# A planned list of instructions: the length over which each engine is held to the plan's order

## The chip, the cores and the metric

The kernel runs on one core of a Trainium2 chip. The metric is the device time of one execution, in microseconds, the median of three runs. The core has five engines with an instruction stream each: TensorE (PE in the profile, its weight loads PEld), VectorE (DVE), ScalarE (ACT), GpSimd (POOL), and SyncE (SP), which issues nearly all DMAs. Each engine works through its own stream in order, and waits on semaphores for the others.

## The reference

Inputs are q, k, v of shape (8, 8, 576, 64) (batch, head, position, width), g_norm of 64, and two weight matrices, 512x2048 and 2048x512. All is float32.

```python
kv  = einsum('bhsd,bhse->bhde', k, v)
out = einsum('bhsd,bhde->bhse', q, kv)
x   = out / sqrt(mean(out * out, -1) + 1e-6) * g_norm      # then heads side by side: (8, 576, 512)
X   = real(fft(fft(x, axis=1), axis=2))
u   = x + X
un  = (u - mean(u)) / sqrt(var(u) + 1e-6)                  # over the last axis
y   = u + maximum(un @ w_ch1, 0) @ w_ch2
```

## The kernel before

Matmuls on TensorE are done in a rounded float32 format, and where that is too coarse each operand is split in a high and a low part and multiplied in three passes (high by high, high by low, low by high). That makes three matmuls out of one in the Fourier and in the feed-forward stages.

The program has two parts. The **first part** takes all eight batches through attention and the Fourier stage, and a share of the feed-forward work along with them. The **second part** does the rest of the feed-forward work in the order in which its loops are written. Only the first part matters here. Its operations, by the names of their PSUM tiles and their lines:

- `ps_k` (L574): k^T v of a head pair, from tiles `km`, `vm` (loads at L553) and the rest rows `kr`, `vr` (loads at L562).
- `ps_q` (L643): q transposed by a matmul with an identity; `qt` is loaded at L618, and one row of it, 2 KB, at L624. ACT copies the result to `fq` (L647).
- `ps_o` (L669): attention output. ACT copies it (L686) and squares it (L691), DVE sums the squares (`ss`, L696), POOL multiplies by the gain (L709).
- the fold: DVE (L774, L785), ACT and POOL (L792, L801) make sums and differences of the rows, and their high and low parts `xh` and `xl`.
- `ps_f` at L816: Fourier over positions, 9 matmuls for each of 4 groups (36 a batch); ACT and DVE copy it to `pt` (L830, L834).
- `ps_f` at L851: Fourier over the width, 36 matmuls a batch; ACT and DVE make `me` and `pm` (L863, L871), POOL adds them to x (L883, L886), SP stores it to `u_scr` (L897).
- `ps_t` (L942): x transposed; ACT and DVE write `unTh` and `unTl` (L951, L954), which SP stores, 1 MB each, to `unT_scr` (L1062).
- `ps_h` (L424) and `acc` (L442): the two feed-forward products, with hidden tiles `hh` (ACT, L434) and `hl` (DVE, L437); a partial result goes to `part_scr` (L1056).
- `ps_s` (L494): spare matmuls, 45 pairs whose result nobody reads, which the plan puts where TensorE would otherwise be idle.

All these take their PSUM tile from one ring of 8 banks, `p8`.

The order is made in two steps. First a `Plan` (class at L92) collects each operation with its engine, a cost in ns, a rank, the operations it comes after and the buffers that it takes from rings. `Plan.run` (L155) then walks through a model of time: whenever an engine is free it takes the ready operation of the lowest rank whose buffers are free, and emits its instructions. Second, the framework's scheduler takes the program that was emitted, and orders each engine's stream anew by its own model of time. What keeps it from this is `Plan.pin` (L129): for every instruction emitted at a planned time up to `PIN_UNTIL` it adds a dependence, without a semaphore, on the last such instruction of the same engine. Instructions emitted later carry no such dependence, and the scheduler may let any of them overtake any other of the same engine, as far as data and buffers allow. `PINNED` names the engines for which it is done: all five. Times in `Plan.run` are ns of the plan's own model, which are not those of the chip: the pinned stretch ends at about 90 us of the trace.

Of the kernel before, what the change touches and what calls it, by code (L numbers as in the profile page):

```python
# [46 lines left out]
SPARE_FROM = 12000  # L47


PIN_UNTIL = 95000  # L50
PINNED = {
    mybir.EngineType.PE, mybir.EngineType.DVE, mybir.EngineType.Activation,
    mybir.EngineType.Pool, mybir.EngineType.SP,
# [35 lines left out]
class Plan:  # L89
# [39 lines left out]
    def pin(self, emit, now):  # L129
# [6 lines left out]
        for i in traced[start:]:  # L136
            if i.engine not in self.pinned or now > PIN_UNTIL:
                continue
# [1298 lines left out]
```

## Time and profile before

| | us |
|---|---|
| median of three runs | 1025.26 |
| lowest, highest | 1024.71, 1025.57 |
| the profiled execution | 1022.79 |
| its span | 1021.0 |
| TensorE busy | 1002.3 (98%) |
| VectorE, ScalarE, GpSimd busy | 475.3, 324.8, 314.4 |

The span is the time from the first to the last instruction that the profile shows; the execution's own time has 1.79 us more. The profile's chain of waits is the path that ended last, followed back from the last instruction to whatever released each step. A window of it lists pieces in order of time, with start, length, engine, tile, line and the count of instructions. The view of waits sums, for an engine's line, the time it stood idle and what ended that. A row with SPq is a DMA being issued; the time in it is that of the issue, not of the transfer. The last store of x in the first part is issued at 327 us of the span; the second part is most of the rest.

### The profile page before, as it was taken

What the parts mean: (1) busy time and instruction counts of PE and PEld (TensorE: products, weight loads), DVE (VectorE), ACT (ScalarE), POOL (GpSimd) and SP (SyncE); (2) the same over time, 40 slices, a digit from 0 to 9 for tenths busy, and PEclk for the clock granted to TensorE, in tenths of its full rate; (3) what the DMA queues carried; (4) which work ended last, traced back from release to release, by engine and by line L of the source; (5) the groups of instructions that cost most, each with busy time, mean ns of one, the idle gap of its engine ahead of it and who ended that gap; (6) DMA issues with size and microseconds to landing.
All of it is one profiled execution on the core that took longest, in us unless ns stands there. A gap on an engine that the chain in (4) does not pass through costs nothing.

```text
span 1021.0 us, 15425 instructions
## 1 busy us (share of the span) xinstructions
PE 1002.3 (98%) x6070; PEld 844.0 (83%) x6070; DVE 475.3 (47%) x847; ACT 324.8 (32%) x657; POOL 314.4 (31%) x328
## 2 busy tenths in 40 slices
PE   5999999999999999999999999999999999999997
PEld 5898888889888888888888888888888888888886
DVE  4897656654788879997131313131221311311211
ACT  2666556554644434344221202121121120210110
POOL 0526768775675132235722303020020010100000
PEclk9999999999999999999999999999999999999999
DMA  9989778664346775645553514230320400400101
GB/s 250 212 230 282 181 209 258 162 170 131 137 163 213 268 253 191 236 129 170 161 179 86 180 59 150 82 125 0 141 67 1 165 21 1 165 0 1 42 1 42
DMA packets 109260, 140.74 MB, mean 138 GB/s; under 512 B 51854, under 2 KB 76482, under 8 KB 104580
## 3 DMA queue, kind: packets, MB, share of 16 engines
q1 hardware_dynamic: 105652, 132.28, 41.9%
q0 software_dynamic: 1920, 6.29, 1.9%
q10 hardware_dynamic: 1616, 1.18, 0.5%
q8 instruction: 48, 0.79, 0.3%
q14 instruction: 24, 0.20, 0.1%
HBM read 88.33 MB, written 51.40 MB: 137 GB/s over the span
## 4 chain that ended last, share of the span: by engine, by line
PE 97%; DMA 1%; ACT 0%; POOL 0%; DVE 0%; issue 0%; SPq 0%; DVEq 0%; POOLq 0%
PE ps_h L424 38%; PE acc L442 38%; PE ps_o L669 4%; PE ps_f L816 4%; PE ps_f L851 4%; PE ps_k L574 3%; PE ps_s L494 2%; PE ps_q L643 2%; PE ps_t L942 2%; DMA qt<-in_q_dram 1%; PE ps_w L383 1%; DMA vm<-in_v_dram 0%; POOL x L883 0%; ACT x L686 0%; DVE uu L1324 0%
## 5 line engine op out<-in xcount | busy, mean ns | idle before, releaser
L424 PE MATMUL ps_h<-unTh,w 128*128 128x512 f32 x1152 | 356.6, 391 | 1.2 <-ACT fq L647 1.2
L442 PE MATMUL acc<-w,hh 128*128 128x512 f32 x1152 | 345.5, 390 | 0.0
L437 DVE SCALAR_TENSOR_TENSOR hl<-ps_h,hh 128x512 fp32r<-128x512 f32 x144 | 99.1, 688 | 371.8 <-ACT hh L434 367.5
L442 PEld LDWEIGHTS acc<-w,hh 128*128 128x128 f32 x1152 | 215.1, 188 | 44.3
L424 PEld LDWEIGHTS ps_h<-unTh,w 128*128 128x128 f32 x1152 | 214.8, 188 | 44.8 <-ACT fq L647 1.4
L434 ACT ACTIVATE hh<-ps_h 128x512 fp32r<-128x512 f32 x144 | 85.8, 596 | 454.0 <-PE ps_h L424 439.2
L424 PE MATMUL ps_h<-unTl,w 128*128 128x512 f32 x576 | 224.3, 389 | 0.0
L442 PE MATMUL acc<-w,hl 128*128 128x512 f32 x576 | 213.5, 389 | 0.0
L424 PEld LDWEIGHTS ps_h<-unTl,w 128*128 128x128 f32 x576 | 108.1, 188 | 22.6
L442 PEld LDWEIGHTS acc<-w,hl 128*128 128x128 f32 x576 | 108.1, 188 | 22.6
L1271 POOL DMA_INDIRECT uu<-u_scr,rowidx x24 | 23.2, 968 | 285.1 <-DVE uu L1324 177.9
L709 POOL TENSOR_TENSOR x<-x,gb 96x512 f32<-96x512 f32 (+1 forms) x42 | 55.0, 1330 | 45.7 <-ACT x L686 40.3
L1290 POOL TENSOR_TENSOR uu<-uu,up 128x512 f32<-128x512 f32 x36 | 45.7, 1298 | 45.2 <-ACT up L1287 45.2
L1234 POOL TENSOR_TENSOR w<-wap,w 128x512 fp32r<-128x512 f32 x18 | 26.4, 1467 | 75.3 <-ACT w L1233 69.1
L669 PEld LDWEIGHTS ps_o<-kvt,fq 64*96 64x96 f32 (+1 forms) x864 | 40.9, 162 | 5.7 <-issue 4.0
L1324 DVE SCALAR_TENSOR_TENSOR uu<-acc,rs_yb,uu 128x512 f32<-128x512 f32 x36 | 25.2, 744 | 42.5 <-PE acc L442 42.5
L669 PE MATMUL ps_o<-kvt,fq 64*96 64x64 f32 (+1 forms) x864 | 44.4, 248 | 0.0
L696 DVE TENSOR_REDUCE ss<-ps_o 96x8 f32<-96x512 f32 (+1 forms) x48 | 32.0, 682 | 26.5 <-ACT ps_o L691 26.3
L792 POOL TENSOR_TENSOR xe<-ab 96x256 f32<-96x256 f32 (+1 forms) x46 | 38.0, 845 | 18.7 <-DVE ab L785 17.9
L816 PE MATMUL ps_f<-cs,xh 96*128 96x290 f32 (+1 forms) x192 | 39.0, 300 | 0.0
L1278 DVE BATCH_NORM_STATS2 bst<-uu 128x6 f32<-128x512 f32 x36 | 24.5, 687 | 29.0 <-DMA uu<-u_scr,rowidx 19.8
L851 PE MATMUL ps_f<-cd,pt 128*96 128x258 f32 (+1 forms) x288 | 37.8, 285 | 0.0
(114 smaller groups left out, 1022.4 us busy)
## 6 DMA issues: line engine op xcount, KB each, us to landing
raw<-in_moe_w_ch_dram SPq DMA_DIRECT2D x32, 512.0 KB
unT_scr<-unTh SPq DMA_DIRECT2D x9, 1024.0 KB
unT_scr<-unTl SPq DMA_DIRECT2D x9, 1024.0 KB
part_scr<-part SPq DMA_DIRECT2D x36, 256.0 KB
unTh<-unT_scr SPq DMA_DIRECT2D x9, 1024.0 KB
unTl<-unT_scr SPq DMA_DIRECT2D x9, 1024.0 KB
up<-part_scr SPq DMA_DIRECT2D x36, 256.0 KB
out_dram<-uu SPq DMA_DIRECT2D x36, 256.0 KB
```

The costliest lines, as they stand in the source:

```text
L424: nc.tensor.matmul(ps, w[c][:, kc * P : (kc + 1) * P], unT[a][:, kc, :], start=(idx == 0), stop=(idx == 3 * KC - 1),)
L434: nc.scalar.activation(hh, ps, AF.Relu)
L437: nc.vector.scalar_tensor_tensor(hl, ps, 0.0, hh.bitcast(F32), ALU.max, ALU.subtract)
L442: nc.tensor.matmul(acc, hpair[a][:, i * P : (i + 1) * P], w[c], start=(first and n == 0), stop=(last and n == 2),)
L574: nc.tensor.matmul(ps.t[s * D : (s + 1) * D, pr * D : (pr + 1) * D], km[:, s, j, :] if j < 4 else kr[:, h, :], vm[:, s, j, :] if j < 4 els ...
L669: nc.tensor.matmul(pss[s].t[:n, at : at + D], fqs[side].t[half, m, :n], kvt.t[half, m], start=True, stop=True,)
L696: nc.vector.tensor_reduce(ss.t[0][:n, :, t, s::2], pss[s].t[:n].rearrange("p (u m e) -> p u m e", u=2, e=D), AX.X, ALU.add,)
L709: nc.gpsimd.tensor_tensor(v_, v_, gb[:n].unsqueeze(1).to_broadcast([n, H, D]), ALU.mult)
L792: nc.gpsimd.tensor_tensor(o[:, s], a[:, 0], a[:, 1], ALU.subtract if s else ALU.add)
L816: nc.tensor.matmul(ps.t[:, :NS], xs[t].t[a][:n, part, ch * P : (ch + 1) * P], cs[:n, part, c, t, :], start=(idx == 0), stop=(idx == 8),)
L851: nc.tensor.matmul(ps.t[:n, :ND], pt.t[a][:, part, ch, offs[t] : offs[t] + n], cd[:, part, c, ch, :], start=(idx == 0), stop=(idx == 5),)
L1290: nc.gpsimd.tensor_tensor(us[j][i], us[j][i], part, ALU.add)
```

## The change

`PIN_UNTIL` goes from 95000 to 260000, so the dependence is added for everything emitted in the first 260 us of the plan's time.

```diff
-PIN_UNTIL = 95000
+PIN_UNTIL = 260000
```

Both programs have the same instructions. Their places differ in one stretch of each engine's stream, on TensorE from about the 605th to the 1870th of 5295, which is about 90 to 267 us of the trace; before and after it the streams are the same.

On TensorE, between the attention products and the next feed-forward block, about 115 us in the trace. Names are those of the list above; `128x97 x4` is the shape of the result and the number of equal instructions in a row. Lines with - are before, with + after:

```order
 L669 MATMUL ps_o<-kvt,fq 96x64 x16
-L574 MATMUL ps_k<-vm,km 64x64 x6
-L942 MATMUL ps_t<-ident,x 128x97 x2
-L942 MATMUL ps_t<-ident,x 128x96 x2
+L942 MATMUL ps_t<-ident,x 128x97 x4
+L942 MATMUL ps_t<-ident,x 128x96 x4
 L643 MATMUL ps_q<-ident,qt 128x96 x4
-L574 MATMUL ps_k<-vm,km 64x64 x2
-L574 MATMUL ps_k<-vr,kr 64x64 x2
-L574 MATMUL ps_k<-vm,km 64x64 x3
-L942 MATMUL ps_t<-ident,x 128x97 x2
-L942 MATMUL ps_t<-ident,x 128x96 x2
```

Before, the products of k and v and the transposes alternate in pieces of two to eight; after, each of them stands whole, the transposes of eight and the ps_k of ten or twenty. A little further on, before, four ps_t stand between the ps_o that follow the acc; after, they stand ahead of the acc. And the last of the 45 spare pairs, which was the last thing ahead of an acc at 90 us, stands between the last two groups of eight ps_q just ahead of the ps_h of 130 us.

On TensorE, in the Fourier stage of the next batch, about 148 us in the trace:

```order
 L851 MATMUL ps_f<-cd,pt_1958 96x258
-L574 MATMUL ps_k<-vm,km 64x64 x2
-L851 MATMUL ps_f<-cd,pt_1957 96x258 x2
-L574 MATMUL ps_k<-vm,km 64x64 x5
-L574 MATMUL ps_k<-vr,kr 64x64 x2
 L851 MATMUL ps_f<-cd,pt_1957 96x258 x2
 L851 MATMUL ps_f<-cd,pt_1958 96x258
```

The ps_k that stood among the 36 matmuls of L851 now come after them, after 16 ps_o and eight ps_t; the 36 stand in one run. The same holds for the 36 at about 181 us.

On SP, at about 204 us in the trace, where two stores of unT (128x2048, 1 MB each) stand next to loads. Before:

```order
L1062 DMA unT_scr<-unTh 128x2048
L1062 DMA unT_scr<-unTl 128x2048
L618 DMA qt<-in_q_dram 96x24x64
L624 DMA qt<-in_q_dram 1x8x64
L553 DMA km<-in_k_dram 128x2x256
L553 DMA vm<-in_v_dram 128x2x256
L1056 DMA part_scr<-part 128x512
```

The same place after the change:

```order
L618 DMA qt<-in_q_dram 96x24x64
L624 DMA qt<-in_q_dram 1x8x64
L553 DMA km<-in_k_dram 128x2x256
L553 DMA vm<-in_v_dram 128x2x256
L1062 DMA unT_scr<-unTh 128x2048
L1056 DMA part_scr<-part 128x512
L1062 DMA unT_scr<-unTl 128x2048
L618 DMA qt<-in_q_dram 96x24x64
```

Here the loads of q, k and v go ahead of the two stores. Elsewhere on SP it is the other way: of the km and vm loads that were issued from 116.9 to 128.2 us ahead of two such stores, four, and vr with them, stand behind the stores after the change.

On DVE, ACT and POOL the moved instructions lie in stretches of about 180, 230 and 135 places; the last copies to `pt` and `pm` go ahead of the next batch's fold on DVE, and the copies of ps_t are not parted any more.

## The prediction

> **What bounds the kernel now.** I read the chain that ended last first, because it names the engine whose time has to shrink. Its share by engine stands on the page:
>
> ```profile
> PE 97%; DMA 1%; ACT 0%; POOL 0%; DVE 0%; issue 0%; SPq 0%; DVEq 0%; POOLq 0%
> ```
>
> TensorE is the chain nearly from end to end, so time can be won only where it stands still or runs slower than it must. The window view shows how much of each stretch it is busy, for the part that was pinned already and for the part that the change pins anew (columns: length, then busy time and count of PE, PEld, DVE, ACT, POOL, the granted clock, DMA share, GB/s):
>
> ```profile
> 20.00:90.40 70.40, 70.40 (x861) 60.24 (x858) 56.62 (x98) 38.77 (x86) 24.50 (x37) 1.00 0.95 245
> 90.40:266.60 176.20, 173.22 (x1703) 151.37 (x1702) 103.15 (x190) 100.61 (x237) 126.04 (x137) 1.00 0.69 191
> ```
>
> In the pinned stretch TensorE is never idle. In the unpinned one it is idle for 176.20 - 173.22 = 2.98 us; the clock is full in both, so no gain or loss can come from it there. The waits of TensorE in that second stretch are three (total, times, longest, us):
>
> ```profile
> PE ps_h L424 <- ACT fq L647: 1.2, 1, 1.2
> PE ps_k L574 <- DMA vm<-in_v_dram: 1.0, 1, 1.0
> PE ps_t L942 <- POOL x L883: 0.4, 1, 0.4
> ```
>
> Plain waiting is thus worth 2.6 us at most. What else can be won lies inside the busy time: an operation that is broken into short pieces takes longer than the same operation in one run. The prices of whole runs come from the chain (start, us, count), at places where nothing breaks them. The trace counts a ps_k matmul twice, so its 60 here are 30 in the program.
>
> ```profile
> 204.34 2.63 PE ps_k L574 x60
> ...
> 209.23 1.50 PE ps_o L669 x32
> ...
> 249.19 1.99 PE ps_t L942 x24
> 251.18 2.40 PE ps_o L669 x32
> 253.58 0.81 PE ps_q L643 x8
> ...
> 285.53 4.30 PE ps_f L851 x36
> ```
>
> **The change part by part.** Instructions and their number stay; only positions move, between about 90 and 267 us of the trace on every engine. So I price the five places where TensorE loses something: the elapsed time in the chain less the same matmuls at the prices above.
>
> **First place, 115 to 131 us:**
>
> ```profile
> 115.33 0.50 PE ps_k L574 x12
> ...
> 121.82 2.09 PE acc L442 x9
> 123.92 0.88 PE ps_o L669 x12
> 124.80 0.48 PE ps_t L942 x4
> 125.28 2.37 PE ps_o L669 x50
> 127.65 0.06 issue
> ```
>
> From 115.33 to 121.82 are 6.49 us, in which eleven pieces alternate: sixty ps_k (2.63), twenty ps_t (1.99 x 20/24 = 1.66) and eight ps_q (0.81), 5.10 in whole runs. So 1.39 are lost in breaks; the new order runs them in seven pieces. From 123.92 to 127.65 are 3.73, for 64 ps_o (3.00) and four ps_t (0.33): 0.40 lost, and the new order has no ps_t between them. Then ps_h waits 1.2 for the bank that the last fq copy frees (the row above). In the new order ps_h waits for another bank, that of the spare matmuls, so this wait goes. What is late next is the pair of ps_q whose banks hang on the square sums (L696) of the two ps_o before them; that is the same evacuation one step earlier, and I count it as covered by the first ps_q and the spare matmuls ahead. Sum 1.39 + 0.40 + 1.2 = 3.0 won.
>
> The spare pair itself:
>
> ```profile
> L494 PE MATMUL ps_s<-still x90: 387/397/588, 13.4 to 90.4; 128*128 128x512 f32 x90
> ```
>
> The last pair goes from 90 us to just ahead of that ps_h. It costs about half a us wherever it stands on the path, so it gives and takes the same: zero. If it stands in a moment when TensorE would wait anyway, half a us more is won.
>
> **Second place, 146 to 165 us:**
>
> ```profile
> 146.32 0.88 PE ps_k L574 x20
> 147.20 1.12 PE ps_f L851 x8
> 148.32 0.26 PE ps_k L574 x2
> ...
> 153.98 0.11 DVE pm L871
> ...
> 164.63 0.40 PE acc L442
> ```
>
> From 146.32 to 153.98 are 7.66 us, for forty ps_k (1.75), 36 ps_f (4.30) and four ps_o (0.19), 6.24 whole: 1.42 lost in breaks. Two ps_k records that stand alone take 0.26 where two sixtieths of 2.63 make 0.09. The new order runs the 36 ps_f as one, so I take back 1.4. From 153.98 to 164.63 are 10.65, for sixty ps_o (2.81), 24 ps_t (1.99), forty ps_k (1.75) and sixteen ps_q (1.62), 8.17 whole: 2.48 lost, and the chain runs through DVE, POOL and ACT there. These engines still have to do the same copies and adds. They start earlier, since ps_f ends earlier, but POOL is nearly full:
>
> ```profile
> 150.00:175.00 25.00, 24.33 (x307) 20.59 (x306) 13.37 (x26) 15.80 (x37) 22.30 (x24) 1.00 0.88 253
> ```
>
> With 22.30 of 25 busy, POOL can close little. Between nothing and 2.48 I take a third, 0.8. Sum of the place: 2.2.
>
> The Trainium skill (TensorE: Matmul & The Clock Gate, Step-by-step: what each phase is for) says that weights for the next tile load while the present matmul streams, by which a break between two independent operations would cost nothing. This trace disagrees: 0.26 for the two ps_k that stand alone, three times their price in a run. By the page the two places would give 1.2 and 0.8 instead of 3.0 and 2.2.
>
> **Third place, 181 to 187 us:**
>
> ```profile
> 180.86 0.38 PE ps_k L574 x6
> ...
> 187.04 0.33 PE ps_q L643 x4
> ```
>
> 6.18 us, for twenty ps_k (0.88) and 36 ps_f (4.30): 1.0 lost. The new order has both whole; I take 0.9.
>
> **Fourth place, 213 to 218 us:** SP issues DMAs in order, and here two loads stand behind a small q load that does not get out:
>
> ```profile
> 206.33 5.89 SPq L624 DMA_DIRECT2D qt<-in_q_dram  x1
> 212.32 1.04 SPq L553 DMA_DIRECT2D km<-in_k_dram  x1
> ```
>
> The vm follows the km. The 5.89 begin right after the two 1 MB stores of unT. The new order puts both q loads and this km and vm ahead of those stores, so vm is issued up to 6 us earlier, against the 1.0 that ps_k waits for it: all of it goes, 1.0.
>
> **Fifth place, 251 us:** ps_o x32 takes 2.40 there (its row stands among the prices), against 1.50 in a whole run: 0.9. The new order alternates its two banks in another way; part may be the wait for copies, so I take 0.7.
>
> The reordering of ACT, DVE and POOL costs nothing in itself: same instructions, same durations. What it can cost is a wait, in order, for something that the free order overtook. No row shows its size; the nearest is the longest wait of TensorE in the stretch, 1.2, and a program order of this length may well contain none or several. I take one: -1.2.
>
> **Sum:** 3.0 + 2.2 + 0.9 + 1.0 + 0.7 - 1.2 = 6.6 us. After 267 us the order is as before and TensorE stays the chain, so the shift is carried to the end. The profiled execution took 1022.79 (span 1021.0) and would take 1016.2 (span 1014.4); the median, 1025.26, lies 2.47 above the profiled time, and I shift it by the same amount: **1018.7 us**. All the losses of the five places together, 3.0 + 3.9 + 1.0 + 1.0 + 0.9 = 9.8, and half a us if the spare pair falls into a wait, bound the gain at 10.3: 1015.0.
>
> **The rivals.** A measurement of this kernel can tell about 0.2%, 2 us, from no change.
>
> *Breaks cost nothing.* Then only the three waits go, 2.6 us: 1022.7. The page named above would have it so. Against it stand 0.26 for two ps_k, and the same ps_f in 4.30 where whole. Chance 0.10, for I might mistake a wait for a bank that the profile does not name for the price of a break.
>
> *POOL sets the pace.* The order gets tighter for TensorE, but POOL is as slow as before, in order now, and TensorE meets it later. The place is the last xl of the fold ahead of 238 us, which ps_f reads:
>
> ```profile
> 233.88 1.29 POOL L801 TENSOR_TENSOR xl<-xe,xh 96x512 fp32r<-96x512 f32 x1
> ```
>
> It ends at 235.17 and the matmuls on it run from about 238.3, so TensorE can come 3.1 us earlier there before it waits, unless POOL comes earlier too. If POOL does not, 3.1 stay; with two new in-order waits of 1.2 some 0.7 stay, and with none of it regained, no change: 1025.3, give or take the 2 us. For it: 22.30 of 25 above, and in the stretch that was pinned before POOL had only 24.50 of 70.40 to do, so its never-idle TensorE proves little for the rest. Against it: POOL's own bursts begin with pm on DVE, which begins with ps_f on TensorE, and that comes earlier. Chance 0.14.
>
> *SP's order makes loads late.* At 118 to 128 us four km and vm loads now stand behind the two unT stores, which stand behind the copies that fill unT.
>
> ```profile
> 129.78 0.44 SPq L1062 DMA_DIRECT2D unT_scr<-unTl  x1
> ...
> 131.73 6.10 SPq L624 DMA_DIRECT2D qt<-in_q_dram  x1
> ```
>
> Here too SP stood for 6.10 after the stores, until 137.83. With the stores 3 us earlier the loads would get through by about 135, and the ps_k that reads the first pair runs at 146.32, or 143.3 in the new order. Four loads of 256 KB and one of 128 KB are 1.2 MB, 6 us at the stretch's 191 GB/s: 141, 2 us to spare for the last, more for the first. It decides from the point where the stores are issued more than 2 us later than that. Then TensorE waits out the stall, 6.1, and once more at the next pair of stores (169 us), where I take half of it, 3.1: 9.2 lost against 6.6 won, 2.6 slower, 1027.9. The Trainium skill (DMA: Bandwidth & Descriptors, Queues, rings and completion order) says that descriptors of one issuing engine's row are consumed in ring order on each DMA engine, which speaks for this rival; the stalls of 5.89 and 6.10 agree. Chance 0.13.
>
> That the change does not do what it says is excluded by the order: the moves are there.
>
> **How the numbers follow.** The forecast has 0.63. Faster by over 0.2%: 0.63, of the first rival 0.06 (1022.7 is 0.25% below), of the second 0.03, together 0.72. Within 0.2%: 0.04 + 0.09 = 0.13. Slower: 0.02 + 0.13 = 0.15. The range goes from the bound of 1015.0 to no change with one new wait of 1.2, 1026.5; the third rival, and little else, lies outside.
>
> **What would show it.** Right: TensorE's waits between 90 and 267 us are under 1.5 us together, ps_f L851 x36 stands as one piece of about 4.3 us at the second and the third place, the ps_h after the acc of the first place starts 3 us earlier than 130.69, the acc of the second place 5 us earlier than 164.63, and ps_h at 266.74 comes at about 260. Wrong, towards POOL: waits of ps_f L816 or ps_t on POOL, with the shift shrinking after 235 us. Wrong, towards SP: waits of ps_k on km or vm near 143 us or near 175. Wrong about breaks: pieces are whole and the elapsed time between the same marks has not shrunk.

## The result, and the profile after

| | before | after |
|---|---|---|
| median, us | 1025.41 (4 runs, 1024.71 to 1027.99) | 1016.93 (4 runs, 1016.69 to 1017.72) |
| ratio, 95% interval | | 0.9915 (0.990 to 0.9931) |
| profiled execution, us | 1022.79 | 1016.69 |
| span, us | 1021.0 | 1014.9 |

The change makes the kernel 8.5 us faster by the medians; 6.6 were forecast. The spans differ by 6.1 only. What follows asks where the 8.5, the 6.1 and the 6.6 come from.

The window view of the kernel after, over the newly pinned stretch (columns as in the prediction: length, then busy time and count of PE, PEld, DVE, ACT, POOL, granted clock, DMA share, GB/s):

```profile
90.40:260.50 170.10, 167.81 (x1712) 148.24 (x1711) 101.09 (x192) 103.82 (x240) 126.82 (x140) 1.00 0.72 199
```

The stretch ends 6 us sooner, while its idle time goes only from 2.98 to 2.29: most of the gain is in what counted as busy. The waits of TensorE over the whole span of the kernel after, but for that of the first load (total, times, longest):

```profile
PE ps_o L669 <- ACT fq L647: 1.3, 1, 1.3
PE acc L442 <- DVE ss L696: 0.6, 1, 0.6
PE ps_q L643 <- DVE ss L696: 0.2, 1, 0.2
```

The three old waits of the stretch (1.2, 1.0, 0.4) are gone, and three new ones have come: 1.3, 0.6, 0.2.

The chain of the kernel after at the first place:

```profile
115.50 0.81 PE ps_t L942 x8
116.32 0.33 PE ps_q L643 x4
116.65 0.88 PE ps_k L574 x20
...
128.50 8.21 PE ps_h L424 x36
```

Every operation stands in one run. ps_k x20 takes its whole-run price of 0.88; ps_t x8 takes 0.81, where the price in the prediction's list makes 0.66, so 0.15 is left for the change of operation ahead of it. At the second place:

```profile
144.76 4.48 PE ps_f L851 x36
...
159.67 4.40 PE acc L442 x18
```

The 36 matmuls of L851 are one run of 4.48. The place still ends with a wait, now for the sum of squares on DVE (the 0.6 above). At the fifth place:

```profile
244.07 1.50 PE ps_o L669 x32
...
250.74 0.03 ACT part L1052
...
251.56 0.38 ACT fq L647
...
260.38 8.41 PE ps_h L424 x36
```

ps_o takes 1.50 instead of 2.40, but the next ps_o waits the 1.3 of the list above: the fq that it reads is copied by ACT, and that copy stands behind the copy of a partial result, which itself waits for the acc that ends just before 250.74. The ps_h that closes the place stands behind ps_o now, where it stood behind acc, and takes 8.41 instead of 8.17.

To compare the two chains place by place, a common start is needed. I take the spare matmuls ahead of 91 us; the kernel before has two pairs there and the kernel after one, and the other pair comes later in its stretch, so the work from there on is the same. Before, then after:

```profile
89.88 0.96 PE ps_s L494 x4
```

```profile
90.92 0.49 PE ps_s L494 x2
```

From there to the ps_h at the end of the stretch are 266.74 - 89.88 = 176.86 us before and 260.38 - 90.92 = 169.46 after: 7.4 won. Up to the next ps_f (L851), 285.53 and 279.40, it is 7.2. That the spans show only 6.1 is decided ahead of 90 us, where the two programs are the same: the kernel after came to this point 1.04 us later.

### The profile page after: what moved, and what is told of

The parts are those of the page before. It is cut to its first block, busy times and chain, and to the rows that moved or that the text cites. A ratio compares the mean times of both kernels' runs of the same rounds, so it can differ in the third digit from the quotient of the medians.

```text
span 1014.9 us, 15420 instructions
## 1 busy us (share of the span) xinstructions
PE 997.5 (98%) x6070; PEld 840.6 (83%) x6070; DVE 472.8 (47%) x847; ACT 326.1 (32%) x657; POOL 313.8 (31%) x328
## 4 chain that ended last, share of the span: by engine, by line
PE 96%; POOL 1%; DMA 1%; ACT 1%; DVE 0%; issue 0%; SPq 0%; DVEq 0%
PE ps_h L424 38%; PE acc L442 38%; PE ps_o L669 4%; PE ps_f L816 4%; PE ps_f L851 3%; PE ps_k L574 3%; PE ps_s L494 2%; PE ps_t L942 2%; PE ps_q L643 2%; DMA qt<-in_q_dram 1%; PE ps_w L383 1%; POOL x L883 0%; POOL x L886 0%; ACT ps_o L691 0%; ACT x L686 0%
## 5 line engine op out<-in xcount | busy, mean ns | idle before, releaser
L669 PEld LDWEIGHTS ps_o<-kvt,fq 64*96 64x96 f32 (+1 forms) x864 | 38.5, 162 | 6.8 <-issue 2.6
L669 PE MATMUL ps_o<-kvt,fq 64*96 64x64 f32 (+1 forms) x864 | 41.6, 248 | 1.3 <-ACT fq L647 1.3
L816 PE MATMUL ps_f<-cs,xh 96*128 96x290 f32 (+1 forms) x192 | 39.4, 300 | 0.0
L851 PE MATMUL ps_f<-cd,pt 128*96 128x258 f32 (+1 forms) x288 | 36.1, 283 | 0.0
```

What stands on the lines that cost most here:

```text
L669: nc.tensor.matmul(pss[s].t[:n, at : at + D], fqs[side].t[half, m, :n], kvt.t[half, m], start=True, stop=True,)
L816: nc.tensor.matmul(ps.t[:, :NS], xs[t].t[a][:n, part, ch * P : (ch + 1) * P], cs[:n, part, c, t, :], start=(idx == 0), stop=(idx == 8),)
L851: nc.tensor.matmul(ps.t[:n, :ND], pt.t[a][:, part, ch, offs[t] : offs[t] + n], cd[:, part, c, ch, :], start=(idx == 0), stop=(idx == 5),)
```

## The experiments

Medians below are to be read against the kernel before as it was measured beside them: 1024.1 (first four runs), 1024.6 (next three), 1024.95 (the two runs with 133000 and 170000).

My theory was that TensorE's own order is what counts; the rival, that it is the order of the engines that copy, and of the loads. The first two runs each keep one half. A table of limits by engine replaces the one limit (`mybir.EngineType.` is left out of the names, and `...` stands for lines in between):

```diff
-PIN_UNTIL = 95000
+PIN_UNTIL = 260000; PIN_FOR = {DVE: 95000, Activation: 95000, Pool: 95000, SP: 95000}
...
-            if i.engine not in self.pinned or now > PIN_UNTIL:
+            if i.engine not in self.pinned or now > PIN_FOR.get(i.engine, PIN_UNTIL):
```

**TensorE alone.**

> Only TensorE is held to the plan's order up to 260; ACT, DVE, POOL and SP stay at 95 as before. Theory (TensorE's own order is what counts: whole runs instead of pieces, and with them most of the waits): the breaks of the first three places go, 1.4 + 0.4 + 1.4 + 0.9 = 4.1 us, and what the other engines bring on top is small: 1017.5 to 1021. Rival (the order of the copying engines and of the loads is what counts, since they free the banks): at most 1.5 us are won, 1024 to 1025.5. The trace tells by the elapsed time from 115 to 131 and from 146 to 165 us.

Measured: 1021.75 us, ratio 0.9981 (0.9972 to 0.999). Only 2.4 us by the medians, outside what the theory gave (1017.5 to 1021) and outside what the rival gave. The program order of TensorE is nearly that of the kernel after, and its pieces are whole; the larger part of what is lost is in the view of waits (the four largest of the eight in the stretch):

```profile
PE ps_f L851 <- DVE pt L834: 1.2, 2, 0.9
PE ps_k L574 <- DMA vm<-in_v_dram: 0.8, 1, 0.8
PE ps_t L942 <- POOL x L886: 0.8, 2, 0.5
PE ps_t L942 <- DVE unTl L954: 0.7, 1, 0.7
...
```

All eight are 5.1 us, where the kernel after has 2.1 and the kernel before 2.6; the 3.0 between this run and the kernel after are most of the 3.4 by which their spans differ (1018.3 and 1014.9). A TensorE in the plan's order meets DVE, ACT and POOL in an order of their own.

**All but TensorE** (the table then holds `PE: 95000` alone).

> The other half: ACT, DVE, POOL and SP are held up to 260, TensorE only up to 95. Theory: TensorE is broken into pieces again, so of 8.5 us only the wait for vm (1.0) and the ps_h wait (1.2) can be won, 1022 to 1025; a TensorE in free order against copying engines in the plan's order may even wait more. Rival: most of the gain is there, 1017 to 1019.

Measured: 1020.02 us, ratio 0.996 (0.9946 to 0.9974), 4.1 us faster. Neither side had it so: the half that I held for the smaller is not smaller. Its trace shows both what it lacks and what it has. Pieces are back at the first place:

```profile
118.96 0.38 PE ps_k L574 x6
119.34 0.32 PE ps_t L942 x2
```

But there are fewer of them: from the spare matmuls to the ps_h that ends the stretch, TensorE changes from one operation to another 105 times, against 111 before and 85 after. That the scheduler orders TensorE better when it finds the copies in the plan's order is how I read this; no run shows it by itself. And a load comes late:

```profile
173.78 8.44 DMA vm<-in_v_dram
```

This vm stands behind both unT stores on SP, lands 8.44 us after its issue, and ps_k waits 0.7 for it. That is the mechanism of the prediction's third rival, at the second pair of stores that it named. In the changed kernel it does not come about, since there ps_k stands behind the 36 ps_f and needs the load later.

**All but SP** (`SP: 95000` alone).

> As the changed kernel, with SP alone left in free order after 95. The streams of the other four engines are the same as in the changed kernel. Theory: only the load of vm at the fourth place is at stake, 1.0 us: 1017 to 1018.5. Rival A (the order of SP is a large part of the gain): over 1019. Rival B (loads behind the big stores cost something in the changed kernel): below 1016.5.

Measured: 1017.07 us, ratio 0.9937 (0.9924 to 0.9951): that of the changed kernel within the noise (medians of 1016.93 and 1016.8). Nor is there a wait for vm in its trace. SP, left free, issues this in the fourth place (all rows are SP's):

```profile
199.60 0.41 SPq L553 DMA_DIRECT2D km<-in_k_dram  x1
200.05 1.54 SPq L553 DMA_DIRECT2D vm<-in_v_dram  x1
201.69 0.41 SPq L1062 DMA_DIRECT2D unT_scr<-unTh  x1
```

The loads go ahead of the stores here too. So this gain is not due to holding SP: with the other four engines in the plan's order, the free order of SP puts these loads first as well.

**The wait at 250 us, twice.** First the limit for all engines goes to 245:

```diff
-PIN_UNTIL = 260000
+PIN_UNTIL = 245000
```

> PIN_UNTIL 245000 instead of 260000: the last 15 us of the plan's time stay free. In the changed kernel's trace ps_o waits 1.3 us at 250.7 for an fq copy that stands on ACT behind a partial result's copy. If it is the pinned order of ACT alone that makes this wait, the free order lets fq overtake and 1.3 us are won: 1015.6. Rival: the free order brings a loss of its own there (0.9 as at the fifth place of before): 1016.9 or above.

Measured: 1015.01 us (1014.79 to 1015.14), ratio 0.9917 (0.9904 to 0.9931). In the same place its chain has no wait:

```profile
246.62 4.16 PE acc L442 x18
250.77 1.50 PE ps_o L669 x32
```

Then ACT alone is let go at 245 (`PIN_FOR = {Activation: 245000}`, the limit at 260000).

> As the changed kernel, but ACT is held only up to 245; DVE and SP keep the changed kernel's streams. If the wait of 1.3 us that ps_o has at 250 us comes from ACT's pinned order alone (the fq copy behind the partial result's copy), the whole gain of the run with 245 for all engines comes back: 1.3 to 2 us below the changed kernel. Rival (it is the pinned order of SP or DVE there, by the time at which banks come free): within 0.5 us of the changed kernel.

Measured: 1015.13 us (1014.77 to 1015.56), ratio 0.9906 (0.9889 to 0.9923), and the changed kernel beside it:

> The changed kernel once more, as the reference for the runs beside it: 1016.5 to 1018, 0.992 of the kernel before.

1016.8 us (1015.74 to 1017.53), ratio 0.9923 (0.9907 to 0.9939). ACT's held order makes the wait: with ACT alone let go, all of the 1.7 us come back. The two kernels with 245 are the fastest of this study, and their runs and those of the changed kernel do not overlap.

**The whole first part.**

```diff
-PIN_UNTIL = 260000
+PIN_UNTIL = 400000
```

> PIN_UNTIL 400000, so the whole first part is held to the plan. After 268 us TensorE was never idle in either kernel and its pieces are whole, so there is nothing left to win: the theory (broken pieces and waits are what counts) expects the time of the changed kernel within 1 us. Rival (a longer hold gains in itself): 2 us or more faster. Second rival (each further stretch brings in-order waits like that of 250 us): 1.3 us or more slower.

Measured: 1021.96 us, ratio 0.9978 (0.9967 to 0.9989): 5.2 us slower than the changed kernel. My theory falls here as well; the second rival is right, and more so than it said. New waits after 268 us:

```profile
PE ps_w L383 <- POOL wp L379: 2.7, 3, 1.2
...
PE ps_o L1131 <- DVE x0h L1123: 1.0, 1, 1.0
```

With one of 0.4 of ps_f (L816) for `wa` on DVE these are 4.1 us in five waits, most of the 5.2. In this stretch weights are prepared on DVE and POOL (`wp`, `wa`); in the chain of this run they come right behind pieces of the fold (DVE, L774 and L785) on their engine. Which engine's held order makes these waits was not separated. The kernels that leave this stretch free have no wait there.

**The price of a break, by itself.** The rival "breaks cost nothing" needs matmuls that wait for nobody, so two small kernels with nothing but such matmuls were profiled, one execution of each.

> A kernel of its own for the price of a break, which computes nothing of the reference: 36 matmuls like those of L851 and 18 like ps_k (two records each), first as two whole runs and then as 6 times (6 and 3), then 18 times (2 and 1); the same with 24 transposes like ps_t. No engine has to wait for another in it. From the second place of before, 1.42 us lost in 8 changes of operation, a change costs 0.18 us: the version in six should take 10 x 0.18 = 1.8 us longer than the whole one, with 18 changes of each kind 6 us longer. Rival (breaks cost nothing, the loss was waiting): under 0.3 us longer.

Window view, each row one version: ps_f and ps_k whole, then in six; ps_t and ps_k whole, then in six; ps_f and ps_k in eighteen. The second figure is the length.

```profile
39.30:44.83 5.53, 5.53 (x74) 5.30 (x72) 0.00 (x0) 0.00 (x0) 0.00 (x0) 1.00 0.01 3
46.42:53.80 7.38, 7.38 (x73) 6.00 (x71) 0.00 (x0) 0.00 (x0) 0.00 (x0) 1.00 0.00 0
55.41:58.60 3.19, 3.19 (x62) 3.01 (x59) 0.00 (x0) 0.00 (x0) 0.00 (x0) 1.00 0.00 0
60.18:65.17 4.99, 4.99 (x62) 3.90 (x59) 0.00 (x0) 0.00 (x0) 0.00 (x0) 1.00 0.00 0
94.20:106.03 11.83, 11.83 (x74) 7.67 (x72) 0.00 (x0) 0.00 (x0) 0.00 (x0) 1.00 0.00 0
```

Ten more changes cost 1.85 us and 1.80, 34 more cost 6.30: 0.18 or 0.19 for each, as read from the trace of before. The profile calls all of it busy.

> As the kernel for the price of a break, with 36 matmuls of 512 columns like ps_h against 18 like ps_k and against 24 transposes, and 36 like L851 against 24 transposes, whole and in six. In the kernel before two ps_t between ps_h cost 0.17 us, their price in a run. If a break is dear only next to short matmuls, the versions with 512 columns take under 0.3 us longer in six, and L851 against transposes 1.8. Rival (each change costs 0.18 whatever stands there): 1.8 us for all three.

Window view again: ps_h and ps_k, ps_h and ps_t, ps_f and ps_t, each whole and then in six.

```profile
12.21:21.56 9.35, 9.35 (x73) 7.61 (x72) 0.00 (x0) 0.00 (x0) 0.00 (x0) 1.00 0.00 0
23.15:34.72 11.57, 11.57 (x74) 7.94 (x72) 0.00 (x0) 0.00 (x0) 0.00 (x0) 1.00 0.00 0
36.30:46.47 10.17, 10.17 (x62) 8.69 (x61) 0.00 (x0) 0.00 (x0) 0.00 (x0) 1.00 0.01 2
47.88:58.34 10.46, 10.46 (x62) 8.63 (x61) 0.00 (x0) 0.00 (x0) 0.00 (x0) 1.00 0.00 0
59.75:66.05 6.30, 6.30 (x62) 6.30 (x61) 0.00 (x0) 0.00 (x0) 0.00 (x0) 1.00 0.01 3
67.46:73.78 6.32, 6.32 (x62) 6.32 (x61) 0.00 (x0) 0.00 (x0) 0.00 (x0) 1.00 0.00 0
```

Both expectations fail. With ps_k the ten changes cost 2.22 us even next to long matmuls; with ps_t they cost 0.29 next to ps_h and 0.02 next to ps_f. So it is neither each change that costs, nor a short neighbour of ps_k or ps_t: of the operations tried here, it is the changes to and from ps_k. The weight loads (PEld) of this trace show a difference. After 512-column matmuls, the first weights of ps_k load when its first matmul starts, after 0.35 us without a load; those of ps_t load 0.23 us ahead of the first matmul:

```profile
24.44 0.31 PEld L293 LDWEIGHTS ps_k<-raw 128*64 128x64 f32 x6 [0.35 <-issue]
24.44 0.45 PE L293 MATMUL ps_k<-raw 128*64 128x64 f32 x6
48.88 0.54 PEld L299 LDWEIGHTS ps_t<-ident,raw 96*128 96x128 f32 x4
49.11 0.50 PE L299 MATMUL ps_t<-ident,raw 96*128 96x96 f32 x4
```

**Place by place.** The limit at 133000, then at 170000.

> PIN_UNTIL 133000: the plan's order covers the first place alone. The sum of the prediction by places gives it 3.0 us: 1021 to 1022 by medians of 1024.1 to 1025.4 for the kernel before; the changed kernel's trace has 3.2 there. Rival (the places are not independent, a hold that ends early gives its gain back at the next free stretch): under 1.5 us.

> PIN_UNTIL 170000: the first two places. The sum of the prediction gives 3.0 + 2.2 = 5.2 us, the trace 3.2 + 2.8 = 6.0: 1018.5 to 1020. Rival as for 133000: under 4 us.

Measured: 1019.93 us, ratio 0.9948 (0.9931 to 0.9965), and 1018.01, ratio 0.9934 (0.9917 to 0.9952). The chains show that each place is won for itself. With 133000 the first place takes what it takes in the changed kernel, 37.58 us from the spare matmuls to its ps_h, and the second is in pieces as before:

```profile
145.30 0.26 PE ps_k L574 x2
145.56 0.88 PE ps_f L851 x6
146.44 0.27 PE ps_k L574 x4
```

With 170000 the second place is whole:

```profile
144.08 4.48 PE ps_f L851 x36
```

Medians fall by 5.0 and 6.9 us, more than the 3.2 and 6.0 of the trace. From the spare matmuls (90.33 and 90.25) to the last ps_h (264.01 and 261.13) the chains of these two take 173.68 and 170.88, so 3.2 and 6.0 less than before's 176.86: the traces give what the places promised, the medians 1 to 2 us on top.

**The kernel before, profiled again.**

> The kernel before, profiled a second time. Its first profiled execution lies 2.5 us below its median, the changed kernel's does not. If the first one was a fast execution, this one has a span near 1023, with the extra time ahead of 90 us (the changed kernel's second profile has its spare matmuls at 13 us in 3.0 instead of 1.9) or in waits between 90 and 268 us; the rival is that the difference lies outside the span.

Measured: 1023.74 us, span 1021.9. Its stretch, spare matmuls to ps_h, is 176.5 us. It is longer by 1.3 us ahead of 90 us, in the spare matmuls at 13 us; the row of this run, and that of the first profile:

```profile
13.66 3.21 PE ps_s L494 x8
```

```profile
13.68 1.92 PE ps_s L494 x8
```

The same eight matmuls took 3.31 in the profile of the kernel after, and between 1.92 and 3.31 in the twelve profiles of this kernel and its variants; the first profile of before has the shortest. It was lucky by 1.3 us at its start, and the span comparison gives the change 1 us too little.

## Why the prediction was right, point by point

The time, 1016.93, lies in the range, 1.8 us below the point. The chains of the two kernels, from the spare matmuls on, give each term of the sum:

| term | forecast | in the traces |
|---|---|---|
| first place (to ps_h) | 3.0 | 40.81 - 37.58 = 3.2 |
| second (to acc) | 2.2 | 2.8 |
| third (to ps_o at 202 us) | 0.9 | 0.8 |
| fourth (to ps_f L851) | 1.0 | 1.4 |
| fifth (to acc) | 0.7 | 0.9 |
| new in-order waits | -1.2 | -1.7 (to ps_h), then -0.2 (in that ps_h) |
| sum | 6.6 | 7.2 |

- **What bounds it.** Right: TensorE stays the chain (96% of it), and the shift is carried on (7.2 at the ps_f of 285 us).
- **The first place.** 3.0 against 3.2, but in part by luck. The seven pieces from 115.50 to 121.23 still take 5.73 us, 0.30 above the whole-run prices, so 1.1 of the 1.39 came back and not all. What made up for it is a run of 32 ps_o just ahead, which the sum did not have. Its rows, before and after:

```profile
113.43 1.89 PE ps_o L669 x32
```

```profile
114.00 1.50 PE ps_o L669 x32
```

Why it was slow before, no run shows. The pair of ps_q that the sum took as covered waits 0.2.

- **Breaks.** Right in size on the whole, and the rival "breaks cost nothing" is refuted by a run. Too wide as a statement: the prediction priced any break. Changes with ps_k have the price, 0.18 to 0.22 us; those between ps_t and ps_f or ps_h have next to none. In the stretch TensorE changes to or from ps_k 40 times before and 24 times after; 16 x 0.18 = 2.9 us. ps_o, of 64 rows, was not measured by itself, but the kernel's own chains price it alike: four ps_t between ps_o took 0.48 in before where they take 0.33 in a run, and nine acc matmuls take 2.11 behind ps_q and 2.26 behind ps_o:

```profile
260.87 2.11 PE acc L442 x9
...
264.48 2.26 PE acc L442 x9
```

Changes to or from either of the two go from 71 to 50. The Trainium skill has both sides. What the prediction cited (TensorE: Matmul & The Clock Gate, Step-by-step: what each phase is for), that the next weights load under the present matmul, agrees with ps_f and ps_t: 0.02 us for ten changes. The Trainium skill (TensorEngine Tiling (Array Packing), Key Properties) also says that a change of tiling mode drains TensorE; ps_k is the operation here that fills 64 columns where ps_f, ps_t and ps_h fill 96 or 128, ps_o the one that fills 64 rows, and their changes cost. That the tile is the cause is argued from this; no run changed it alone. A rival stands beside it: ps_k and ps_o are also the two that move 64 columns only. Against that one speak the weights of ps_k above, which load late behind matmuls of 512 columns.
- **The second place.** The third of the 2.48 us that I took was too little. Of 3.9 us lost from 146.32 to 164.63, 2.5 came back (the same work takes 15.78 from 143.89 to 159.67, where whole runs make 14.41); the prediction had 2.2. Another 0.2 comes in the ps_h just ahead, 8.21 instead of 8.46.
- **The fourth place.** The size is right, the reason half right. The loads are issued ahead of the stores, but not because SP is held: SP left free does the same. And part of the wait was TensorE's free order, which wanted ps_k after 18 of the 36 ps_f.
- **One new in-order wait.** Right in kind and size: 1.3 us, and shown to be ACT's held order. The rest of the -1.7 and the -0.2 are not waits but runs of ps_o, acc and ps_h that take longer in the new order. And the sign that I had named, waits under 1.5 us together, did not come true: they are 2.1, with 0.6 and 0.2 for the square sums on DVE.
- **The POOL rival.** The chain touches POOL, as it said, and TensorE waits there a little. In the kernel after, chain and weight load:

```profile
226.98 1.26 POOL xl L801
228.24 0.04 issue
228.28 4.01 PE ps_f L816 x28
```

```profile
228.28 0.19 PEld L816 LDWEIGHTS ps_f<-cs,xl 96*128 96x128 f32 x1 [0.33 <-POOL xl L801]
```

The waits of the matmuls have no row for this, that of the weights has: 0.33 us. The slack of 3.1 us was read from the old order, in which the matmuls on this xl stood near the end of the 36; in the plan's order the ninth reads it. What kept the loss small is that POOL's bursts came earlier by nearly as much as TensorE (this xl began at 233.88 before, 6.9 later). Whatever more is gained ahead of it would be lost here, unless POOL comes earlier too.

- **The SP rival** does not occur in the changed kernel; the run without TensorE's hold shows it, at 0.7 us and not at 9.
- **What I had not said.** I argued the case as one of TensorE's order. The halves show 2.4 us for TensorE alone and 4.1 for the others alone, all five together about 8: the gain lies in the engines following the same plan.

What stays open: the medians give 8.5 us, or 7.8 where both kernels were measured again (medians of 1024.6 and 1016.8), and the traces 7.2. Both profiled executions of the kernel before (1022.79, 1023.74) lie below its medians (1024.1 to 1025.4); those of the changed kernel are nearer to theirs (1016.69 against 1016.93, 1016.31 against 1016.8). The kernel before also varies more: its runs go from 1021.69 to 1028.87, those of the changed kernel from 1015.74 to 1017.72. A profile shows one execution out of such a spread, and the two of before fell into its lower part. The run with 133000 has already gained the difference (5.0 by medians, 3.2 in the trace), so it may lie in the stretch that this run pins, but no run shows where.

## What to carry to other kernels

A planned order is best held on all engines together: half of it, on either side, gave 2.4 and 4.1 us of about 8 here, and left waits or broken runs. Hold it only as far as it pays, and read where that ends from the waits: a held engine whose copy stands behind one that is itself late (ACT at 250 us, and by the waits DVE and POOL after 268 us) gives some of the gain back, and letting ACT alone go 15 us of the plan's time earlier was worth 1.7 us. A loss need not be a wait: look in the busy time for runs of matmuls that take longer in pieces than in one.

## What the runs showed of the hardware that was not expected

A change between ps_k (fp32, weights of 128 rows by 64 columns) and another operation costs TensorE 0.18 to 0.22 us, which the profile counts as busy; a change between ps_t (fp32, weights of 96 rows by 128 columns) and ps_f or ps_h costs 0.002 to 0.03. Behind 512-column matmuls the weights of ps_t load 0.23 us ahead of its first matmul, those of ps_k only with it. And the same eight 512-column matmuls at 13 us took from 1.92 to 3.31 us in twelve profiles, at a granted clock that the window view gives as 1.00 in all of them: the start of a run can differ by 1.4 us between executions.
